# Cutting the last 256 bytes of each row of a weight load into sixteen small loads of 15 to 1 partitions

## The chip, the cores and the metric

The kernel runs on one core of a Trainium2 chip. The metric is the device time of one launch in microseconds (us); the time before is the median of three runs, 186.52 us.

## What is computed

Attention for one new token in each of 32 sequences, over a window of the last 512 cached positions:

```python
W = min(4096, max(256, Sk // 4))          # 512
q = (x @ wq) -> 32 sequences x 32 heads x 128
k = k_cache[:, :, Sk - W:, :]             # 8 key heads, each for 4 query heads
v = v_cache[:, :, Sk - W:, :]
p = softmax(q . k * Dh ** -0.5)
out = (p . v) as 32 x 4096, @ wo          # wo: 4096 x 512
```

All arrays are bfloat16. x is 32 x 512, wq 512 x 4096, wo 4096 x 512. The windows of k_cache and v_cache are 33.6 MB each, wq and wo 4.2 MB each: the 75.5 MB that the profile shows as read.

## The kernel before

The work goes in eight steps of four sequences (q = 0 to 7 in the code). For a step the core loads 4 MB of keys (`K_sb`, two buffers) and 4 MB of values (`V_sb`, two buffers), turns the keys on VectorE, makes scores on TensorE, the softmax on ScalarE and VectorE, and the products with the values on TensorE. Three texts at the top of the file, `PE_OPS`, `DVE_OPS` and `ACT_OPS`, give each engine its operations in an order written out by hand; `needs` names what each one waits for.

SyncE (SP) issues all the large loads, on one queue, in the order of `LOADS`: keys and values of all steps and, last, W0, W1 and W2, the three parts of wo. They go to the first key buffer (`wo_sb` is `K_sb[0]`) and wait only until that buffer is free. Partition p of `wo_sb` holds rows 32p to 32p + 31 of wo, 32 KB in one piece. `WOP` cuts each partition's 32 rows into 16, 12 and 4, that is 16, 12 and 4 KB in each partition, each part with its own semaphore `sem_wo[q]` (lines 239 to 245). After these, SP waits for the result and issues the output's store (lines 246 to 251).

x comes on ScalarE's queue in four loads of 2, 6, 10 and 14 rows (`X_PARTS`, lines 186 to 189).

At the end TensorE waits for the last `D` (line 385) and multiplies by wo, 32 rows of each partition, four column blocks: 64 matmuls after W0, 48 after W1, 16 after W2 (lines 386 to 400). It waits for one semaphore ahead of each group:

```python
for j, (i0, i1) in enumerate(WOP):
    pe.wait_ge(sem_wo[j], 16)
```

The last group's results are copied by VectorE and ScalarE (lines 479 and 528) and stored by SP.

Of the kernel before, what the change touches and what calls it, by code (L numbers as in the profile page):

```python
# [38 lines left out]
X_PARTS = [(0, 2), (2, 8), (8, 18), (18, 32)]  # L39
V_PIECES = [1, 1, 1, 1, 1, 2, 2, 4]  # L40
WOP = [(0, 16), (16, 28), (28, 32)]


def ops_of(text):
    return [(w[0],) + tuple(int(n) for n in w[1:].split(".")) for w in text.split()]


def bass_standalone__sliding_block_cached__sampling_kernel(
# [7 lines left out]
):  # L56
    B, Sq, D = x.shape
    _, HKV, SK, DH = k_cache.shape
    HD = wq.shape[1]
    HQ = HD // DH  # L60
# [9 lines left out]
    NI = 32  # L70
# [49 lines left out]
    with ExitStack() as es:  # L120
        sb = lambda name, shape, dt: es.enter_context(nc.sbuf_tensor(name, shape, dt))
        sem = lambda name: es.enter_context(nc.semaphore(name))
# [24 lines left out]
        wo_sb = K_sb[0][:, :].rearrange("p (i n) -> p i n", i=NI)  # L147
# [19 lines left out]
        sem_k = [sem(f"sem_k{i}") for i in range(2)]  # L167
        sem_v = [[sem(f"sem_v{i}_{j}") for j in range(max(V_PIECES))] for i in range(2)]
        sem_wo = [sem(f"sem_wo{i}") for i in range(len(WOP))]
        sem_out = sem("sem_out")  # L170
        names = (
            "pe_xT pe_q pe_Y dve_xT dve_q dve_QT dve_m dve_r dve_y dve_c act_q act_y act_warm "
# [18 lines left out]
        def load_wq(i):  # L191

            nc.sync.dma_start(
                wq_sb[:, 2 * i:2 * i + 2, :].rearrange("p k n -> p (k n)"),
                wq.rearrange("(p k) n -> p k n", k=DKT)[:, 2 * i:2 * i + 2].rearrange("p k n -> p (k n)"),
            ).then_inc(sem_wq[i], 16)
# [4 lines left out]
        def rows(cache, q, r0=0, r1=R):  # L201
            return cache[4 * q:4 * q + 4, :, SK - W:, :].rearrange(
                "b h (k r) d -> (b h) k (r d)", k=KB)[:, :, r0 * DH:r1 * DH]
# [14 lines left out]
        @block.sync  # L218
        def _(sp):
            wait = Waits(sp)  # L220
            load_wq(1)
            wo_r = wo.rearrange("(p i) n -> p i n", i=NI)
            for op in ops_of(" ".join(LOADS)):
                kind, q = op[0], op[1]
                if kind == "K":
                    if q >= 2:
                        wait([ends["T", q - 2, 1]])
                    sp.dma_start(K_sb[q % 2][:, :], rows(k_cache, q)).then_inc(sem_k[q % 2], 16)
                elif kind == "V":
                    if q == 1:  # L230
                        sp.wait_ge(s["pe_q"], 8)
                    if q >= 2:
                        wait([ends["P", q - 2, 31]])
                    n = R // V_PIECES[q]
                    r0 = op[2] * n
                    sp.dma_start(  # L236
                        V_sb[q % 2][:, r0 * DH:(r0 + n) * DH], rows(v_cache, q, r0, r0 + n)
                    ).then_inc(sem_v[q % 2][op[2]], 16)
                else:
                    wait([ends["T", NQ - 2, 1]])  # L240
                    i0, i1 = WOP[q]
                    sp.dma_start(  # L242
                        wo_sb[:, i0:i1, :].rearrange("p i n -> p (i n)"),
                        wo_r[:, i0:i1, :].rearrange("p i n -> p (i n)"),
                    ).then_inc(sem_wo[q], 16)
            sp.wait_ge(s["dve_y"], 2)
            sp.wait_ge(s["act_y"], 2)
            sp.dma_start(
                out.rearrange("b s n -> b (s n)"), out_sb[:, :, :].rearrange("b c n -> b (c n)")
            ).then_inc(sem_out, 16)  # L250
            sp.wait_ge(sem_out, 16)
# [44 lines left out]
        def _(pe):  # L296
# [88 lines left out]
            wait([ends["D", NQ - 1]])  # L385
            for j, (i0, i1) in enumerate(WOP):
                pe.wait_ge(sem_wo[j], 16)

                last = i1 == NI
                for cs in ((0, 1), (2, 3)) if last else ((0, 1, 2, 3),):  # L390
                    for i in range(i0, i1):
                        for c in cs:
                            ins = pe.matmul(  # L393
                                Y_ps[32 * c:32 * (c + 1), 0:P],
                                lhsT=o_sel[:, i, :],
                                rhs=wo_sb[:, i, c * P:(c + 1) * P],
                                start=i == 0, stop=i == NI - 1, tile_position=(0, 32 * c),
                            )
                    if last:
                        ins.then_inc(s["pe_Y"], 1)  # L400
# [158 lines left out]
```

## Time and profile before

| | |
|---|---|
| median of three runs | 186.52 us (186.37 to 186.85) |
| profiled execution | 186.74 us |
| its span in the profile | 185.0 us |
| TensorE busy (matmuls) | 119.9 us, 65% of the span |
| VectorE busy | 106.5 us, 58% |
| ScalarE busy | 49.7 us, 27% |
| read from HBM | 75.53 MB, 409 GB/s over the span |
| issue to landing of the three parts of wo | 18.8, 21.8, 22.6 us |
| chain that ended last: DMA, VectorE, TensorE | 59%, 22%, 9% |

The profile is one execution. PE is TensorE, PEld its loading of weights, DVE VectorE, ACT ScalarE, POOL GpSimd, SP SyncE; a small q behind a name (SPq) is that engine's instruction queue. Times in the views count from the start of the span; L393 is line 393 of the kernel. A group's line gives start and duration, then engine, line, operation, the tile written and the tiles read, and in brackets the idle time before it with what ended it. The granted clock is TensorE's, as a share of full speed. Semaphore waits are not counted as busy. A DMA is carried by up to 16 DMA engines, each with its own row of packets, and each engine adds one to the DMA's semaphore when its share has landed; whole DMAs wait for 16.

### The profile page before, as it was taken

To read this page: it belongs to the slowest core of one execution; us is meant where nothing else is said; L and a number is where in the kernel's file an instruction comes from. 1 tells how busy PE (TensorE), PEld (TensorE's weight loads), DVE (VectorE), ACT (ScalarE), POOL (GpSimd) and SP (SyncE) were. 2 spreads that over 40 slices of the span, in tenths; PEclk is the share of its full clock that TensorE was granted. 3 is DMA by queue.
4 is the path that set the end of the run, shared out by engine and by line. 5 is a ranking of instruction groups with operands and counts; after the bars stand their busy time and mean duration, and the time that the engine had idled before them with its cause. 6 is when DMAs were issued, how large, how long until landed. Compare 5 with 4: busy or idle time off the path is not lost.

```text
span 185.0 us, 3664 instructions
## 1 busy us (share of the span) xinstructions
PE 119.9 (65%) x1636; PEld 56.3 (30%) x1636; DVE 106.5 (58%) x106; ACT 49.7 (27%) x93; POOL 16.9 (9%) x52
## 2 busy tenths in 40 slices
PE   0089104447696597649934994342799899898943
PEld 0024000013453153314421351001345446354542
DVE  0031999994549524972298328999637996320201
ACT  3000300012925037301650154001062715420301
POOL 7900040202000110001000200020000000000000
PEclk9999965556999799687995599655569999999996
DMA  6998999999999999999999999999999999999960
GB/s 213 421 500 369 432 454 454 454 390 404 450 454 443 411 386 454 454 436 425 392 436 454 432 418 411 439 446 439 418 411 411 429 425 425 411 420 431 431 287 27
DMA packets 3872, 75.80 MB, mean 410 GB/s; under 512 B 464, under 2 KB 528, under 8 KB 656
## 3 DMA queue, kind: packets, MB, share of 16 engines
q1 hardware_dynamic: 3792, 75.53, 95.9%
q8 instruction: 13, 0.21, 0.5%
q10 hardware_dynamic: 64, 0.03, 0.1%
q14 instruction: 3, 0.02, 0.0%
HBM read 75.53 MB, written 0.03 MB: 409 GB/s over the span
## 4 chain that ended last, share of the span: by engine, by line
DMA 59%; DVE 22%; PE 9%; issue 6%; SPq 2%; ACTq 1%; DVEq 0%
DMA K_sb<-in_k_cache_dram 43%; DVE KT_sb L445 17%; DMA K_sb<-in_wo_dram 12%; PE ps L313 4%; PE ps L361 4%; DMA bd<-in_x_dram 4%; DVE QT_sb L437 2%; DVE KT_sb L434 1%; SPq L236 1%; DVE C_sb L470 1%; ACTq L187 1%; SPq L242 1%; PE ps L331 1%; DVE bd L413 0%; PE ps L393 0%
## 5 line engine op out<-in xcount | busy, mean ns | idle before, releaser
L445 DVE STREAM_TRANSPOSE KT_sb<-K_sb 128x4096 f32<-128x4096 f32 x16 | 70.5, 4431 | 9.7 <-DMA K_sb<-in_k_cache_dram 9.6
L361 PE MATMUL ps<-V_sb,bd 32*128 32x512 bf16 x1024 | 64.1, 402 | 4.3 <-DMA V_sb<-in_v_cache_dram 1.7
L331 PE MATMUL ps<-KT_sb,QBD 128*32 128x512 bf16 x256 | 26.0, 544 | 39.0 <-DVE KT_sb L445 29.8
L361 PEld LDWEIGHTS ps<-V_sb,bd 32*128 32x128 bf16 x1024 | 27.4, 98 | 38.3 <-issue 14.7
L331 PEld LDWEIGHTS ps<-KT_sb,QBD 128*32 128x32 bf16 x256 | 6.7, 115 | 55.6 <-DVE KT_sb L445 36.9
L496 ACT ACTIVATE P_f<-ps,negmax 128x512 f32<-128x512 f32 x8 | 5.5, 687 | 62.3 <-DVE negmax L453 62.3
L509 ACT ACTIVATE bd<-PTc,mask 128x512 bf16<-128x512 bf16 x31 | 20.1, 711 | 0.3
L514 ACT ACTIVATE C_sb<-ps 32x512 f32<-32x512 f32 x22 | 12.9, 587 | 23.7 <-PE ps L361 23.5
L289 POOL COPY QBD<-QT_sb 32x128 bf16<-32x128 bf16 x32 | 9.2, 287 | 106.6 <-PE ps L331 89.9
L465 DVE TENSOR_SCALAR bd<-PTc,mask 128x512 bf16<-128x512 bf16 x33 | 9.3, 348 | 15.3 <-ACT PTc L503 15.3
L470 DVE COPY C_sb<-ps 32x512 f32<-32x512 f32 x10 | 6.9, 693 | 14.5 <-PE ps L361 14.4
L373 PE MATMUL ps<-C_sb,F_sb 128*128 128x128 f32 x64 | 9.7, 298 | 5.6 <-ACT C_sb L514 5.0
L373 PEld LDWEIGHTS ps<-C_sb,F_sb 128*128 128x128 f32 x64 | 8.2, 200 | 8.4 <-ACT C_sb L514 7.2
L346 PE MATMUL ps<-P_bf,E_sb 128*128 128x128 bf16 x128 | 9.8, 237 | 1.1 <-DVE P_bf L459 1.1
L451 DVE TENSOR_REDUCE maxv<-ps 128x1 f32<-128x512 f32 x8 | 5.5, 687 | 8.4 <-PE ps L331 8.4
L503 ACT ACTIVATE PTc<-ps 128x512 bf16<-128x512 f32 x8 | 4.7, 593 | 19.6 <-PE ps L346 19.6
L346 PEld LDWEIGHTS ps<-P_bf,E_sb 128*128 128x128 bf16 x128 | 8.3, 107 | 5.1 <-DVE P_bf L459 2.5
L313 PE MATMUL ps<-V_sb,bd 128*128 128x512 bf16 x32 | 9.1, 453 | 0.8 <-DVE bd L413 0.8
L301 PE MATMUL ps<-bd 32*128 32x128 bf16 x4 | 0.6, 295 | 8.9 <-DMA bd<-in_x_dram 8.9
L434 DVE CAST KT_sb<-ps 128x512 bf16<-128x512 f32 x4 | 2.5, 682 | 6.5 <-PE ps L313 6.5
L413 DVE CAST bd<-ps 128x512 bf16<-128x512 f32 x1 | 0.7, 692 | 9.5 <-PE ps L301 9.5
L490 ACT ACTIVATE KT_sb<-ps 128x512 bf16<-128x512 f32 x4 | 2.1, 603 | 14.3 <-PE ps L313 14.3
(29 smaller groups left out, 34.3 us busy)
## 6 DMA issues: line engine op xcount, KB each, us to landing
K_sb<-in_k_cache_dram SPq DMA_DIRECT2D x8, 4096.0 KB, 25.6
V_sb<-in_v_cache_dram SPq DMA_DIRECT2D x5, 4096.0 KB, 29.4
V_sb<-in_v_cache_dram SPq DMA_DIRECT2D x4, 2048.0 KB, 20.2
V_sb<-in_wq_dram SPq DMA_DIRECT2D x2, 2048.0 KB, 9.8
V_sb<-in_v_cache_dram SPq DMA_DIRECT2D x4, 1024.0 KB, 11.8
K_sb<-in_wo_dram SPq DMA_DIRECT2D x1, 2048.0 KB, 18.8
K_sb<-in_wo_dram SPq DMA_DIRECT2D x1, 1536.0 KB, 21.8
K_sb<-in_wo_dram SPq DMA_DIRECT2D x1, 512.0 KB, 22.6
```

The costliest lines, as they stand in the source:

```text
L289: pool.tensor_copy(QBD[pr, q % 2].rearrange("p (w t) (h c) -> p w t h c", w=2, h=HKV)[:, :, :, :, 4 * b:4 * b + 4], QT_sb[pr, q].rearrange ...
L313: ins = pe.matmul(ps[:, n], lhsT=xT_sb[:, kt, :], rhs=wq_sb[:, kt, n * 512:(n + 1) * 512], start=kt == 0, stop=kt == DKT - 1, tile_positio ...
L331: ins = pe.matmul(S_ps[32 * c:32 * c + 32, :], lhsT=QBD[:, q % 2, 2 * w + t, c0:c0 + 32], rhs=KT_sb[:, w, :, KB * h:KB * h + KB, t], start ...
L346: ins = pe.matmul(EP_ps[:, e * R:(e + 1) * R], lhsT=E_sb[:, k, e].rearrange("p m j -> p (m j)"), rhs=P_bf[:, k * R:(k + 1) * R], start=k = ...
L361: ins = pe.matmul(O_ps[:, b, :], lhsT=bd[pr, q % 2, 4 * g:4 * g + 4].rearrange("p r h e -> p (r h e)"), rhs=V_sb[q % 2][pr, 512 * g:512 * ...
L373: ins = pe.matmul(F_ps[:, 0:P], lhsT=F_sb[:, d].rearrange("p h d -> p (h d)"), rhs=C_sb[:, q % 2, :, 32 * d:32 * d + 32], start=d == 0, st ...
L445: return dve.transpose(KT_sb[:, w].bitcast(F32).rearrange("p r c t -> p r (c t)"), K_sb[q % 2][:, :].bitcast(F32).rearrange("p (r w c) -> ...
L451: dve.tensor_reduce(maxv[:, q:q + 1], S_ps, AX.X, ALU.max).then_inc(s["dve_m"], 1)
L465: ins = dve.tensor_scalar(o, i, m, None, op0=ALU.mult)
L470: ins = dve.tensor_copy(*pick_args(q, r))
L509: ins = act.activation(o, i, ACTF.Copy, scale=m)
L514: ins = act.activation(*pick_args(q, r), ACTF.Copy)
```

## The change

The last 256 bytes (128 elements) of each partition's rows of wo leave the load W2. They come by sixteen loads issued right behind it on SP, over 15, 14, 13, 12, 11, 10, 9, 8, 8, 7, 6, 5, 4, 3, 2 and 1 partitions (128 in all), each with a semaphore of its own. TensorE waits for all of them, in the opposite order, ahead of its last 16 matmuls.

```diff
+WO_LAST = 128
+WO_GROUPS = (15, 14, 13, 12, 11, 10, 9, 8, 8, 7, 6, 5, 4, 3, 2, 1)
...
+        sem_wl = [sem(f"sem_wl{i}") for i in range(len(WO_GROUPS))]
...
                     i0, i1 = WOP[q]
-                    sp.dma_start(
-                        wo_sb[:, i0:i1, :].rearrange("p i n -> p (i n)"),
-                        wo_r[:, i0:i1, :].rearrange("p i n -> p (i n)"),
-                    ).then_inc(sem_wo[q], 16)
+                    n = (i1 - i0) * D - (WO_LAST if i1 == NI else 0)
+                    dst = wo_sb[:, i0:i1, :].rearrange("p i n -> p (i n)")
+                    src = wo_r[:, i0:i1, :].rearrange("p i n -> p (i n)")
+                    sp.dma_start(dst[:, :n], src[:, :n]).then_inc(sem_wo[q], 16)
+                    if i1 == NI:
+
+                        p0 = 0
+                        for g, np_ in enumerate(WO_GROUPS):
+                            sp.dma_start(
+                                dst[p0:p0 + np_, n:], src[p0:p0 + np_, n:]
+                            ).then_inc(sem_wl[g], 16)
+                            p0 += np_
...
                 pe.wait_ge(sem_wo[j], 16)
+                if i1 == NI:
+                    for g in reversed(range(len(WO_GROUPS))):
+                        pe.wait_ge(sem_wl[g], 16)
```

## Prediction

> **What bounds the kernel now.** I read the chain that ended last, then the stretch around its end in order of time, then the DMA share over that stretch. In the chain (start, duration, what):
>
> ```profile
> 159.09 22.60 DMA K_sb<-in_wo_dram
> 181.69 0.04 issue
> 181.74 0.63 PE ps L393 x15
> 182.37 0.02 issue
> 182.39 0.28 DVE P_bf L479
> ```
>
> The last step of the kernel begins when the third part of wo has landed, at 181.69. The timeline shows three groups of output matmuls, each behind its part of wo:
>
> ```profile
> 177.33 1.08 PE L393 MATMUL ps<-K_sb,o_sel 128*32 128x128 bf16 x64 [0.37 <-ACT o_sel L518]
> 180.50 0.85 PE L393 MATMUL ps<-K_sb,o_sel 128*32 128x128 bf16 x48 [2.09 <-DMA K_sb<-in_wo_dram]
> 181.74 0.64 PE L393 MATMUL ps<-K_sb,o_sel 128*32 128x128 bf16 x16 [0.38 <-DMA K_sb<-in_wo_dram]
> 183.04 0.36 SPq L248 DMA_DIRECT2D out_dram<-P_bf  x1
> ```
>
> From the first matmul of the last group (181.74) to the end of the span (185.0) there are 3.2 us that nothing here shortens: what moves 181.74 moves the end. The windows view (the last three columns are granted clock, DMA share, GB/s) shows that this wait is not one for bandwidth:
>
> ```profile
> 177.00:178.00 1.00, 0.67 (x48) 0.67 (x52) 0.00 (x0) 0.28 (x1) 0.00 (x0) 1.00 0.95 397
> 178.00:179.00 1.00, 0.41 (x32) 0.23 (x20) 0.00 (x0) 0.00 (x0) 0.00 (x0) 1.00 0.59 242
> 179.00:180.00 1.00, 0.00 (x0) 0.00 (x0) 0.00 (x0) 0.00 (x0) 0.00 (x0) 1.00 0.39 160
> 180.00:181.00 1.00, 0.50 (x36) 0.50 (x40) 0.00 (x0) 0.00 (x0) 0.00 (x0) 1.00 0.24 98
> 181.00:182.00 1.00, 0.62 (x40) 0.44 (x32) 0.00 (x0) 0.00 (x0) 0.00 (x0) 0.79 0.11 29
> ```
>
> From 178 us on most of the 16 DMA engines have nothing left, and a quarter of them (0.24) work on. The landings that the trace holds for the last part say the same, one per engine: five at 178.4 to 178.7, three at 179.2 to 179.5, four at 180.0 to 180.1, four at 181.37, 181.62, 181.64, 181.69. What makes them late is in the page's queue table:
>
> ```profile
> q8 instruction: 13, 0.21, 0.5%
> ```
>
> Thirteen blocks of 16 KB of TensorE's program; in the packet records each stops one engine for 1.0 to 1.1 us. Twelve come before the end; eight engines had one each, and the last four fetches (151.1, 160.9, 167.1, 175.7 us) hit four engines a second time. Those four are the late ones.
>
> **Which engines they are decides this change.** The four x loads have 2, 6, 10 and 14 rows and leave 64 packets, 32 of 1024 B and 32 semaphore writes, so n rows go to n engines, one row each. Following each engine's packets (the next starts 4 ns before the last one's recorded end), two engines carry no x row, four one, four two, the others more: the sets are nested. I number the engines by it, e0 in every set, e14 and e15 in none. The late engines, traced back from 181 to 5 us: two are among e10 to e13. The third is among e0 to e5, unless it was swapped with one of e10 to e13 that ran 1 to 2 ns beside it from 8 to 18 us. The fourth I can't resolve (e6 to e9, or below).
>
> **Part 1: 256 bytes off each row of the last part.** A 4096 B row takes 155 ns to the next, a 12288 B row 456, so 0.0367 ns per byte and 5 ns fixed. Each engine has 8 rows, which end 8 x 9.4 = 0.08 us earlier: -0.08 us on the landing of the third part.
>
> **Part 2: 16 small loads.** e0 gets 16 rows of 256 B, e5 11, e7 9, e8 7, e10 5, e13 2, e15 none, each followed by a 4 B semaphore write (6 ns from start to start). No 256 B packet is in the trace. By the line above one takes 14 ns; the nearest row is 1024 B, 46 ns. So 20 to 50 ns for each pair; I take 30, nearer to the line, because packets of 1024 to 32768 B lie on it. Below 20 it can't go much: the semaphore write alone is 6. An engine among e0 to e5 is then busy 0.33 to 0.48 us longer for 0.08 saved.
>
> The Trainium skill (DMA: Bandwidth & Descriptors, Specifications) has transfers under 512 B do a read-modify-write; if that doubled the 14 ns, a pair would be 34 ns, which is an estimate from that page, and the sum below would move by 0.03 us. The same page (Latency and other measured facts) says that engines 7 and 15 are usually the slower ones, and puts it to software-generated rings. If e15 were the late one, the change would gain its 0.08 us; if e7 were, it would be as bad as any low engine. The trace has neither as a standing laggard: lateness there goes with the instruction fetches.
>
> Issuing: SP issues one large load in 0.43 to 0.59 us, ACT the 6- to 14-row x loads in 0.27 to 0.35. Sixteen more at 0.27 to 0.59 keep SP until 164 to 169 us. Nothing else is queued on SP before the output load's waits at 183, and the third part lands at 181.7, so over 9 us cover it: nothing. Without that cover it would be 4 to 9 us.
>
> **Part 3: 16 more waits on TensorE.** The built program has them ahead of the first matmul of the last group: the load of its weights carries the wait for the third part, and before it come wait instructions with two semaphores each, in the order (7,8), (6,9), (5,10), (4,11), (3,12), (2,13), (1,14), (0,15). So eight instructions, and the output group is queued behind them. The trace has such instructions back to back:
>
> ```profile
> L216 PEldq EVENT_SEMAPHORE  x17: 51/51/51, 46.5 to 175.7; - x17
> ```
>
> They last 51 ns, but start 106 to 111 ns apart where nothing holds them (146.799 and 146.910; 166.857 and 166.963), and the weight load behind starts 77 ns after the last (167.040). All eight with every semaphore there: 7 x 0.107 + 0.077 = 0.83 us. TensorE's queue runs ahead of the array by 20 weight loads (20 were still to start after the wait instructions at 71.162, 139.910 and 153.764), so the first could run when 28 of the 48 loads of the second group are done, at 180.88, and the last group could start at 181.71, not later than now. The eight are hidden if none is held.
>
> They are held by order. The first pair needs the loads of 8 rows, on e0 to e7, and only then do the other seven run. If a late engine is among e0 to e7, its ninth small row is needed first: 181.69 - 0.08 + 9 x 0.03 = 181.88, plus 0.045 from landing to release as now (181.69 to 181.735), plus 0.83 = 182.75. Against 181.735 this is +1.0 us. With 20 and 50 ns a pair: +0.93 and +1.2. If the lowest late engine is e10, the fourth pair, (4,11), is the first held; the landing is 181.61 + 5 x 0.03 = 181.76, and 4 x 0.107 + 0.077 follow: 182.31, +0.6. If it is e13, the seventh pair is the first held: +0.15.
>
> Sum, likeliest case: profiled span 185.0 + 1.0 = 186.0, and 1.74 us around it (186.74 - 185.0) make 187.74. The profiled execution lies 0.22 over the median of the runs, 186.52, so 187.5 for the median. The vector and scalar copies and the output's transfer move along unchanged; the clock is already 0.50 from 181.57 on, so the matmuls are not slower than now.
>
> **Rivals.**
> 1. A late engine among e0 to e7: 187.4 to 187.7. For it: the third late engine as traced, and the fourth possibly. Against: the swap I can't exclude. 0.55.
> 2. The lowest late engine is e8 to e13: +0.15 to +0.8, so 186.7 to 187.3. For it: two of the late ones are traced there. 0.25.
> 3. Not slower: the late engines are at the top, e14 and e15, because the fetches go round the engines from another starting place in other executions. Then the waits pass early and only the -0.08 remains, 186.45. It decides from the point where every late engine carries at most one small row. 0.12, with some 0.03 for a clear gain that I see no source of, other than a fetch that no longer falls on a late engine (one fetch less there is about -1.1 us).
> 4. Slower still: the thirteenth fetch, at 181.76 now, falls on an engine that has small rows left, or SP's longer program brings one more fetch on a late engine; 1.1 us more, 188.6. For it: the same engine was done only 0.5 us before that fetch. Against: the ninth row is through by 181.6 even at 50 ns. 0.08.
>
> That the change doesn't do what it says can be left out: the built program shows the 16 loads and the waits.
>
> **How the numbers follow.** About 0.3%, 0.56 us, is what a measurement of this kernel can tell from no change: 186.0 to 187.1. Slower takes case 1, a quarter of case 2 (a late e8 or e9, above 187.1) and case 4: 0.55, 0.06 and 0.08 make 0.69. Faster 0.04. The rest, 0.27, is the same. The range leaves out case 4 and the clear gain: from 186.4 (case 3) to 187.9 (case 1 with 50 ns a pair and 0.2 for the spread between runs). Case 1's own range is 187.3 to 187.9.
>
> **What would show it.** In the changed profile: the third part's landing near 181.6; 128 packets of 256 B; eight wait instructions on TensorE at 0.107 us, the first released at 181.8 to 182.0; the last group of output matmuls at 182.7; SP done issuing by 169. Wrong if the last group starts within 0.1 us of its own landing (then the waits cost nothing, case 3), if the small rows take over 50 ns, or if the late engines are not the ones with two fetches.

## The result and the profile after

The changed kernel is slower: 189.87 us (188.47 to 190.45, four runs) against 186.51, a ratio of 1.0162 (95% interval 1.0132 to 1.0193). A second comparison gave 189.44 us and 1.0163 (1.0121 to 1.0205). The prediction was 187.5 us with a range to 187.9: the direction is right, the loss is more than three times the one forecast. The profiled execution took 189.33 us, its span 187.5, that is 2.5 us more than before.

The chain of the changed kernel (start, duration, what) ends through a small load:

```profile
163.87 0.29 SPq L254
164.16 0.04 issue
164.21 19.43 DMA K_sb<-in_wo_dram
183.63 0.72 issue
184.36 0.63 PE ps L408 x15
```

The DMA from 164.21 is the load over 7 partitions. It lands at 183.63, and 0.72 us pass before the last matmuls, where there were 0.04. In the timeline everything ahead of that stands within 0.3 us of where it stood, and the last group starts 2.6 us later (184.36 for 181.74):

```profile
159.74 6.69 SPq L254 DMA_DIRECT2D K_sb<-in_wo_dram  x16
180.66 1.19 PE L408 MATMUL ps<-K_sb,o_sel 128*32 128x128 bf16 x48 [1.97 <-DMA K_sb<-in_wo_dram]
184.36 0.64 PE L408 MATMUL ps<-K_sb,o_sel 128*32 128x128 bf16 x16 [2.51 <-DMA K_sb<-in_wo_dram]
```

What is peculiar is seen in the windows (after the stretch and its length: granted clock, DMA share, GB/s):

```profile
180.00:181.00 1.00, 1.00 0.24 97
181.00:182.00 1.00, 0.51 0.14 30
182.00:183.00 1.00, 0.50 0.00 0
183.00:184.00 1.00, 0.50 0.00 0
```

From 182 us on the loads move nothing: the last data or semaphore packet of them ends at 181.42. (The view counts a packet where it starts; one engine still carries the thirteenth block of TensorE's program, from 181.81 to 183.16.) TensorE waits until 183.6 for loads whose packets are long through. The landings tell how that goes. In the trace the last landing of the 9-, 8-, 8- and 7-row loads is at 183.02, 183.23, 183.43 and 183.63: steps of 0.20 us, on one engine, which carries one row of 256 B and one increment of each. An increment is the one that an engine adds to the load's semaphore. The packets of that engine's loads follow each other in 20 ns (18 ns recorded for the 256 B, 9 for the increment).

The wait instructions on TensorE (minimum, median, maximum in ns, first and last start):

```profile
L402 PEldq EVENT_SEMAPHORE  x8: 51/51/209, 183.3 to 184.2; - x8
```

The first of the eight, for the two 8-row loads, is over at 183.465; the second is held until 183.666 by the 7-row load; the last starts at 184.250, the weight load at 184.326: 0.86 us for the chain after the first, 0.09 of them the second's wait.

**Which engines are late.** With nested loads the landings count them: the 6-row load has none after 182.5 us, the 7-row load one (so e6), the 10-row load two of the late kind (e9), the 11-row load three (e10), the 12-row load four (e11). e6, e9, e10 and e11 are late, in this profile and in the next two of the same kernel. The packet records agree: behind the last large rows of the four engines stand ten, six, five and four small ones.

### The profile page after: what moved, and what is told of

It is laid out like the page before. It is cut to its first block, busy times and chain, and to the rows that moved or that the text cites. A ratio compares the mean times of both kernels' runs of the same rounds, so it can differ in the third digit from the quotient of the medians.

```text
span 187.5 us, 3688 instructions
## 1 busy us (share of the span) xinstructions
PE 119.8 (64%) x1636; PEld 57.8 (31%) x1636; DVE 106.6 (57%) x106; ACT 49.9 (27%) x93; POOL 16.9 (9%) x52
## 4 chain that ended last, share of the span: by engine, by line
DMA 69%; DVE 13%; issue 6%; SPq 5%; PE 5%; DVEq 0%
DMA K_sb<-in_k_cache_dram 59%; DVE KT_sb L460 12%; DMA K_sb<-in_wo_dram 10%; PE ps L373 4%; SPq L254 2%; SPq L240 1%; DVE C_sb L485 1%; SPq L249 1%; PE ps L343 1%; SPq L197 0%; PE ps L408 0%; SPq L232 0%; DVE maxv L466 0%; DVEq L123 0%; DVE P_bf L494 0%
## 5 line engine op out<-in xcount | busy, mean ns | idle before, releaser
L373 PE MATMUL ps<-V_sb,bd 32*128 32x512 bf16 x1024 | 63.3, 398 | 3.8 <-DMA V_sb<-in_v_cache_dram 1.9
L343 PE MATMUL ps<-KT_sb,QBD 128*32 128x512 bf16 x256 | 25.3, 532 | 39.2 <-DVE KT_sb L460 29.6
L358 PE MATMUL ps<-P_bf,E_sb 128*128 128x128 bf16 x128 | 11.0, 254 | 0.8 <-DVE P_bf L474 0.8
L358 PEld LDWEIGHTS ps<-P_bf,E_sb 128*128 128x128 bf16 x128 | 9.3, 115 | 4.9 <-DVE P_bf L474 2.8
L325 PE MATMUL ps<-V_sb,bd 128*128 128x512 bf16 x32 | 8.6, 438 | 0.8 <-DVE bd L428 0.8
L408 PE MATMUL ps<-K_sb,o_sel 128*32 128x128 bf16 x128 | 2.9, 249 | 4.8 <-DMA K_sb<-in_wo_dram 4.5
```

Of the source, the lines that this page charges most:

```text
L325: ins = pe.matmul(ps[:, n], lhsT=xT_sb[:, kt, :], rhs=wq_sb[:, kt, n * 512:(n + 1) * 512], start=kt == 0, stop=kt == DKT - 1, tile_positio ...
L343: ins = pe.matmul(S_ps[32 * c:32 * c + 32, :], lhsT=QBD[:, q % 2, 2 * w + t, c0:c0 + 32], rhs=KT_sb[:, w, :, KB * h:KB * h + KB, t], start ...
L358: ins = pe.matmul(EP_ps[:, e * R:(e + 1) * R], lhsT=E_sb[:, k, e].rearrange("p m j -> p (m j)"), rhs=P_bf[:, k * R:(k + 1) * R], start=k = ...
L373: ins = pe.matmul(O_ps[:, b, :], lhsT=bd[pr, q % 2, 4 * g:4 * g + 4].rearrange("p r h e -> p (r h e)"), rhs=V_sb[q % 2][pr, 512 * g:512 * ...
```

## The experiments

Theory S: increments from one DMA engine land 0.17 to 0.20 us apart, however short the packets, and the late low engine's row of them decides; the eight wait instructions add 0.8 us because they are held by the first of them. (The prediction's e0 to e15 number the engines by how many of the nested loads they carry.) Rivals: the wait instructions themselves (W), the small data (D, R), engines that stand still (B), a spread with a cause other than which engines are late (V).

**One semaphore for all sixteen loads.**

```diff
-                            ).then_inc(sem_wl[g], 16)
+                            ).then_inc(sem_wl[0], 16)
...
-                    for g in reversed(range(len(WO_GROUPS))):
-                        pe.wait_ge(sem_wl[g], 16)
+                    pe.wait_ge(sem_wl[0], 16 * len(WO_GROUPS))
```

> All sixteen small loads count up one semaphore (16 x 16 = 256), so one wait instruction stands ahead of the last group in place of eight. Theory S (each small load's increment lands 0.17 to 0.20 us after the one before it on the same engine, though its packets take 20 ns): the last landing stays where it is, 2 to 3 us after the third part's, and only the 0.75 us of the seven other wait instructions goes: 189.0 to 189.4. Rival W (the wait instructions on TensorE are the cost): 186.6 to 186.9.

188.11 us, ratio 1.0086 (1.0058 to 1.0114). W alone is out: 1.4 us over the kernel before remain with a single wait instruction. But it is 1 us less than S had expected. In the profile, which is that of the quickest of six runs (187.52), the last landing came at 182.54, 1.03 us after the third part's (181.51), which is six increments of 0.17, not the ten of e6. Either increments to one semaphore are quicker, or e6 was not late there. The packet records say the second: behind the last large rows of the four late engines stand six, five, four and three small rows, so they are e9 to e12. The two kernels with loads of 16 rows, below, test the same without that reading.

**The same bytes in one load.**

```diff
-WO_GROUPS = (15, 14, 13, 12, 11, 10, 9, 8, 8, 7, 6, 5, 4, 3, 2, 1)
+WO_GROUPS = (128,)
```

> The same 256 bytes of each row come by one load over 128 partitions: per engine eight 256 B packets and one increment, in place of 0 to 16 of both. Theory S: one increment more per engine, the last group +0.1 to +0.3 us after that of before: 186.5 to 186.9. Rival D (it is the 256 B data writes that land slowly, 0.19 us each): 8 x 0.19 = 1.5 us on every engine: 187.9 to 188.2.

187.06 us, ratio 1.0029 (1.0011 to 1.0047). Every engine writes eight 256 B rows and one increment; the small load's last landing, 181.84, is 0.16 us after the third part's. D is out: the rows don't take 0.19 us each. The last group starts here:

```profile
181.97 0.64 PE L408 MATMUL ps<-K_sb,o_sel 128*32 128x128 bf16 x16 [0.49 <-DMA K_sb<-in_wo_dram]
```

This is the cheapest form of the cut, and still a loss.

**Eight loads of 16 rows, with eight semaphores and with one.**

```diff
-WO_GROUPS = (15, 14, 13, 12, 11, 10, 9, 8, 8, 7, 6, 5, 4, 3, 2, 1)
+WO_GROUPS = (16,) * 8
```

> Eight loads over 16 partitions in place of the sixteen nested ones: every engine carries eight 256 B rows and eight increments. Theory S: the last landing is 181.6 + 8 x 0.19 = 183.1 whichever engines are late; the last wait instruction needs it, so the last group starts at 183.2 to 183.4: 188.0 to 188.3, and the runs differ by no more than those of before (0.5 us). Rival V (which engines are late does not change from run to run): the spread of the changed kernel, 2.0 us, has another source and stays.

> The eight loads over 16 partitions again, all counting up one semaphore (128). In the first shared-semaphore run the last landing came 1.0 us after the third part's, not 2: late e6 would then have had its ten increments 0.10 us apart in place of 0.17 to 0.20. Theory S1 (increments to different semaphores wait longer for each other than increments to one): here every engine carries eight, the last landing is 0.8 us after the third part's, the last group starts at 182.5: 187.2 to 187.6. Rival S2 (the interval is the same, other engines were late in that run): the last landing 1.4 us after the third part's, as with eight semaphores, the start at 183.2: 187.9 to 188.2.

188.64 us, ratio 1.0105 (1.0074 to 1.0136), and with one semaphore 188.41 us, 1.0098 (1.0079 to 1.0116). The rows of each engine are those of the single load, but they come as eight loads with eight increments, not as one with one. With eight semaphores the last group starts here:

```profile
183.31 0.64 PE L408 MATMUL ps<-K_sb,o_sel 128*32 128x128 bf16 x16 [1.91 <-DMA K_sb<-in_wo_dram]
```

against 181.97 with the single load. The first engine's landings come at 178.44 (third part), 178.62, 178.79, 178.96, 179.13, 179.30, 179.46, 179.64, 179.82: 0.17 us apart. With one semaphore the last landing is 1.43 us after the third part's, 0.18 for each, so S2 holds and S1 falls: the semaphore does not matter. The spans of the four runs with eight semaphores lie within 0.4 us (186.1 to 186.5), those of the changed kernel within 2.0 (186.7 to 188.7). That fits S, since with the same load on every engine it is of no account which are late; but the times of these runs spread over 1.0 us (188.02 to 189.04), twice what S had expected.

**1024 B in place of 256 B.**

```diff
-WO_LAST = 128
+WO_LAST = 512
```

> The same sixteen nested loads with 1024 B in place of 256 B of each row (the third part's rows shrink to 3072 B). Theory S: increments on one engine still land 0.17 to 0.20 us apart, since 1024 B take 46 ns only; the third part lands 0.3 us earlier and the rest as in the changed kernel: 188.3 to 190.3. Rival R (writes under 512 B are slow to land): the interval falls to 0.05 to 0.1 us and the time to 187.2 to 188.2.

189.42 us, ratio 1.0118 (1.0077 to 1.0159). The last landings of the 8-, 8- and 7-row loads are at 183.24, 183.44 and 183.65, 0.20 us apart as with 256 B; a packet is now 46 ns. R is out: with rows four times as long the landings are no closer.

**The small loads ahead of the first part of wo.**

```diff
+                    if q == 0:
...
+                        for g, np_ in enumerate(WO_GROUPS):
+                            sp.dma_start(
+                                la[p0:p0 + np_], lb[p0:p0 + np_]
+                            ).then_inc(sem_wl[g], 16)
+                            p0 += np_
                     sp.dma_start(dst[:, :n], src[:, :n]).then_inc(sem_wo[q], 16)
-                    if i1 == NI:
...
```

> The sixteen small loads are issued ahead of the first part of wo, so 20 us before they are needed; loads, semaphores and TensorE's waits are the same. Theory S: the landings lag behind unseen, the eight wait instructions run while the second group's matmuls are queued, the last group starts with the third part's landing: 186.4 to 186.9. Rival W: still +0.8 us for the waits, 187.2 to 187.5. Rival B (an engine stands still while its increments land): e0 loses 16 x 0.19 = 3 us of transfer time: 187.5 to 189.5, and the third part lands later.

188.31 us, ratio 1.0078 (1.0055 to 1.01). S fails here: the kernel is slower, though all small loads have landed by 172.70, over 8 us before TensorE's first wait (181.20). Of B one half is seen: the engines lose time just behind the small loads. First the windows of this kernel, then the same stretches of the kernel before (granted clock, DMA share, GB/s):

```profile
169.00:170.00 1.00, 1.00 1.23 376
170.00:171.00 1.00, 1.00 0.97 345
171.00:172.00 1.00, 1.00 1.04 371
```

```profile
169.00:170.00 1.00, 1.00 1.10 467
170.00:171.00 1.00, 1.00 0.91 385
171.00:172.00 1.00, 1.00 1.04 442
```

The DMA share is as high or higher, the bytes are fewer. In the packet records the 16 KB rows behind the small loads last up to 1.97 us, where 0.61 is usual; the excess over all of them is 12.5 us, or 0.10 us for each of the 128 rows. So with large rows behind them about half of each landing's interval comes back as lost time. The other half of B is not seen. The profile is that of the quickest of the nine runs (187.04), and in it the third part lands at 181.67, no later than before (181.69); what is late is the last group:

```profile
180.56 1.47 PE ps L409 x48
182.03 0.02 issue
182.05 0.62 PE ps L409 x15
```

The clock was halved from 180.55 on (from 181.57 in the kernel before), and the second group took 1.47 us where it had taken 0.85. The 1.7 us by which the median is slower are in no profile; that in those runs the lost time fell on late engines is argued, not shown.

**The wait instructions without the loads.**

```diff
-                    n = (i1 - i0) * D - (WO_LAST if i1 == NI else 0)
+                    n = (i1 - i0) * D - 0
...
-                            sp.dma_start(
-                                dst[p0:p0 + np_, n:], src[p0:p0 + np_, n:]
-                            ).then_inc(sem_wl[g], 16)
...
+            for g in range(len(WO_GROUPS)):
+                pool.wait_ge(*((sem_wl[g - 1], 1) if g else (s["pool_qbd"], 4 * NQ)))
+                pool.memset(junk2[:, g:g + 1], 0.0).then_inc(sem_wl[g], 1)
...
-                        pe.wait_ge(sem_wl[g], 16)
+                        pe.wait_ge(sem_wl[g], 1)
```

GpSimd counts the semaphores up behind its last copy of the queries, long before the end.

> The third part of wo is whole and there are no small loads; the sixteen semaphores are counted up by GpSimd long before the end, and TensorE's eight wait instructions stay. Theory S: they run while the second group's matmuls are queued, at 0.106 us each: 186.5 to 186.9, at most +0.35 where the clock is halved during that group. Rival W: +0.8 us, 187.3 to 187.5.

186.79 us, ratio 1.003 (0.9995 to 1.0064). Wait instructions and last group in this kernel's profile:

```profile
L398 PEldq EVENT_SEMAPHORE  x8: 51/51/51, 180.9 to 181.7; - x8
181.78 0.43 PE L404 MATMUL ps<-K_sb,o_sel 128*32 128x128 bf16 x16 [0.43 <-DMA K_sb<-in_wo_dram]
```

They run from 180.93 to 181.67, beside the second group, and the last group starts where it did. Four of the twelve runs lie at 188.7 to 189.5; no profile shows one of these, and why is open. They have no small loads, so a spread of 2 to 3 us does not need them. By its interval alone this comparison does not exclude 0.8 us; the profile does for the execution that it shows.

**The changed kernel twice more.**

> The changed kernel once more. Theory S with late engines that differ from run to run: its landings count the late engines by number (n rows land on e0 to e(n-1)); the lowest late one, if at most e7, holds the first pair of waits until its ninth increment, so the last group starts at 181.6 + 9 x 0.19 + 0.8 = 184.1 or later; with the lowest at e10 it is 181.6 + 5 x 0.19 + 0.5 = 183.1. Time 188.3 to 190.5, spread over 1 us. Rival V: the same late engines as in the first profile (e6, e9, e10, e11), and a spread with another source.

> A third profile of the changed kernel. As for the one before: the late engines' numbers are read from the landings and the start of the last group follows from the lowest by the same sum. Rival V: e6, e9, e10, e11 again.

189.44 us and 189.29. The last group starts at 184.12 and 184.33 after landings of the 7-row load at 183.40 and 183.60, and the late engines are e6, e9, e10 and e11 both times. In the three profiles of this kernel V, that they don't change, held; the kernel with one semaphore (e9 to e12) already spoke against it.

**The waits in the order of landing.**

```diff
-                    for g in reversed(range(len(WO_GROUPS))):
+                    for g in (9, 7, 5, 3, 1, 10, 12, 14, 15, 13, 11, 0, 2, 4, 6, 8):
```

The built program takes such a list in pairs from its middle outwards: here (14,15), (12,13), (10,11), (0,1) and so on to (8,9).

> The changed kernel with the same loads and semaphores; TensorE's wait instructions take them in the order in which the lowest late engine, e6, lands them: first those without it, then (0,1) to (8,9). Seven instructions then run before the last landing, and only the last one after it: the last group starts 0.10 to 0.15 us after that landing, in place of 0.9 (0.86 for the wait instructions). 0.7 us less than the changed kernel by the profile: 188.4 to 189.2. Rival: if the order is of no account, as the changed kernel, 189.3 to 189.9.

189.36 us, ratio 1.0127 (1.0098 to 1.0155): no gain beyond the intervals. The profile is that of the quickest run, 187.94 us; the other three lie at 189.22 to 189.64 and have none:

```profile
L402 PEldq EVENT_SEMAPHORE  x8: 51/51/549, 181.3 to 183.1; - x8
183.18 0.43 PE L408 MATMUL ps<-K_sb,o_sel 128*32 128x128 bf16 x16 [1.82 <-DMA K_sb<-in_wo_dram]
```

Here e6 was not late: the 10-row load has no landing of the late kind, the 11-row load one, the 14-row load four. The late engines are e10 to e13, with five rows and fewer. V falls: the set does change, here with the same loads and semaphores. What held the waits was the 6-row load, on e5, at 182.56: an engine that is not among the four late ones but carries eleven small rows, and whose load stands in the third pair; from its release at 182.60 to the weight load at 183.15 the five instructions behind it cost 0.55 us.

**Half of the third part moved to the low engines**, an attempt to use what the landings had told:

```diff
+                    if i1 == NI:
+                        cuts = [(0, P, 0, n // 2), (0, 114, n // 2, n), (114, P, n // 2, n)]
...
```

> The kernel before with its third part of wo in three loads on one semaphore: 2 KB of all 128 rows, 2 KB of 114 rows, which no number from 7 to 16 divides, and 2 KB of 14 rows. If the 114 go to e0 to e5 (19 rows each) the late engines (e6, e9, e10, e11 in four profiles) carry 9 half rows or 8 and not 8 whole ones: they end 0.55 us earlier, while e5, the latest of the six, ends at 181.2. The last group starts 0.3 to 0.5 us earlier: 186.1 to 186.4. Rival: the late engines are others in most runs, or each added increment costs its engine 0.1 us more: 186.6 to 187.0.

188.18 us, ratio 1.0076 (1.005 to 1.0102). It does not pay. The second part of wo, which was not touched, lands at 181.31 in place of 180.46, and the third at 182.49. Neither the set of late engines nor 0.1 us for an increment makes that 0.85 us; its cause is open. Two things differ in the packet records and no run separates them: from 177.3 us on, when the half rows run beside them, rows of the second part last 475 to 760 ns (460 to 472 before, but for one of 925 beside a block of TensorE's program), and the twelfth block of that program comes at 179.52 us, not at 175.65. No version that I ran beats the kernel before.

## Why the prediction was right or wrong

**What bounds the kernel** was read rightly: the last landing sets the end, and 3.2 us follow it as before (184.36 to 187.5 is 3.1).

**Part 1** gave 0.08 us that can't be seen: the third part landed at 181.76 in the changed profile, 181.69 before.

**Part 2 is the step that failed.** It said "20 to 50 ns for each pair; I take 30". That is the time for which an engine is busy, and as such it was right (20 ns). But the sum in part 3 used it as the step from landing to landing, "181.69 - 0.08 + 9 x 0.03 = 181.88". The runs showed 0.20 us in its place. e6 is the third of the late engines to end its large rows, and the third of their landings is at 181.63 (the one at 181.76 is that of e9); its ninth increment landed at 183.43, 1.80 us later. The term is nearly seven times too small, 1.53 us of the 1.58 by which the first weight load of the last group (182.75 forecast, 184.33 measured) was missed. With 0.20 the sum reads 181.63 + 1.80 + 0.035 + 0.86 = 184.33. The trace of before had no two short loads in a row at an end that mattered, and the bound above was taken from packets, not from landings. One hint was there: the last row of the third part ends at 181.25, and lands at 181.69.

The time itself was missed by more, 2.4 us (187.5 for 189.87). The profiled execution has 1.6 of it (187.74 for 189.33), which is the step above. The rest is that the median of the four runs lies 0.5 above the profiled one, where 0.2 below was forecast; it comes from the two runs at 190.4, and no profile shows such a run.

**Part 3** held: eight instructions in the order of the built program, 0.106 us apart, 0.86 us in all for 0.83 forecast, behind the first pair. Only that the second pair would be held once more, by the tenth increment, was left out. That they are hidden when nothing holds them was right too (first at 180.93, forecast 180.88). So was the cover for SP's issuing: it ended at 166.4.

**Rivals.** Case 1 (a late engine among e0 to e7) came true through e6. I had the third late engine among e0 to e5, with a note that it might have been swapped. In no profile of nested loads is one of e0 to e5 among the four; as the set differs between executions, that does not show which it was in the trace of before. Case 1 held through an engine that I had only as a possible fourth. Case 3, that other executions have other late engines, is real (the profiles with e9 to e12 and e10 to e13), but not as a gain, since e9 carries six increments and e10 five. Case 4, one more instruction fetch on a late engine, is not what the profile shows: the thirteenth came at 181.81, behind the last packet of the loads. The 2 us between the runs fit late engines that differ: e6 gave 189.1 to 189.3, e10 with a better order 187.9. But the kernel without small loads spreads as far in four of twelve runs, and what the runs at 190.4 to 190.8 had is not shown by any profile.

## What to carry to other kernels

Count a transfer at the end by when its semaphore lands, not by how long its packets occupy an engine: here each further DMA on an engine put its landing 0.17 to 0.20 us later, as much as about 5 KB of data (at the 0.0367 ns per byte of the large rows). Cutting the last transfer into many, to even out engines by a few hundred bytes, saves nanoseconds and costs tenths of microseconds; and engines that end 3 us behind the first ones are not evened out by 2 KB. The wait instructions cost nothing that the profile shows while the queue still had work ahead of them (180.93 to 181.67, in the kernel with the wait instructions alone), and their full row of 0.106 us each once the first of them was held.

## What the runs showed of the hardware

Increments of successive DMAs on one DMA engine land 0.17 to 0.20 us apart when their packets follow each other in 20 to 50 ns. It is the same with 256 B and 1024 B, with sixteen semaphores, eight and one. One DMA with eight 256 B rows on each engine lands 0.16 us after the third part. Each of these DMAs had both a row and an increment, and no run separates the increment from the rest of what a DMA brings. Where 16 KB rows followed 128 such increments, the rows lasted 12.5 us longer in sum, about 0.10 us for each increment.

The Trainium skill (DMA: Bandwidth & Descriptors, section on the anatomy of one DMA, which describes DMAs issued by GpSimd) calls the bubble of a semaphore write on trn2 about one cycle, essentially free. Among the packets it is small here too (the next one starts 6 ns later); for the landings of these DMAs, issued by SP, it is not so, and the 0.17 to 0.20 us measured here decide. The same page (on why a DMA increments its semaphore by 16) has each engine's increment as a strongly ordered write that lands only after that engine's data. This may be the reason; that the writes wait for each other's receipts is argued, not shown.

Which engines end late is not fixed: e6, e9, e10, e11 in four profiles with nested loads, e9 to e12 in the one with a single semaphore, e10 to e13 in a sixth. That instruction fetches make them late is the prediction's reading of the trace before (each fetch stops one engine for 1.0 to 1.1 us); no run here changed the fetches.
